# Finer early fill products and another order of the first batch's products, in strided sparse attention followed by a Mish MLP

## The chip, the cores and the metric

The kernel runs on one core of one Trainium2 chip. The metric is the device time of one execution in microseconds (us). The time before is the median of five runs. Where the text speaks of TensorE, VectorE, ScalarE, GpSimd and SyncE, the profile writes PE (and PEld for its weight loads), DVE, ACT, POOL and SP.

## The reference

Eight batches of eight heads, 576 positions, 64 values a head. Heads 0 to 3 attend to the last 32 positions ("local"), heads 4 to 7 to the earlier positions that are equal to their own modulo 32 ("strided"). The result, 4608 rows of 512, goes through an MLP with 2048 hidden values.

```python
scores = scale * np.matmul(q, k.transpose(0, 1, 3, 2))          # scale = 1/8
mask_local = (rel >= 0) & (rel < 32)                            # heads 0..3
mask_strided = (rel >= 0) & (pos[None, :] % 32 == pos[:, None] % 32)   # heads 4..7
attn = softmax(np.where(mask, scores, -1e9))
x = np.matmul(attn, v).transpose(0, 2, 1, 3).reshape(4608, 512)
h = x @ w_in                                                    # 512 -> 2048
g = h * np.tanh(np.log1p(np.exp(h)))                            # Mish
out = g @ w_out                                                 # 2048 -> 512
```

## The kernel before, in words

All data for the products is bf16, sums are fp32 in PSUM. The order of instructions on each engine is written out by hand. The MLP works on nine blocks of 512 rows: `mlp1` (line 575, then Mish at 581) makes the hidden values, `mlp2` (line 599) the output. While the MLP of block t runs, the attention of batch t+1 is put between its products. The first batch has nothing to lie beside, so its attention is a piece of its own at the start (lines 677 to 722), and this is the piece that the change touches.

The steps of this piece, in the old order:

- **Fills.** `fill` (line 547) issues products of a zeroed tile, whose result nobody reads. They keep TensorE busy while loads, copies and exponentials are on their way. Every product in this kernel, fills too, is one weight load and one matmul.
- **Transposes.** `t_step` (237) turns keys and queries of the strided heads, two heads in a step; VectorE copies the first step's result out of PSUM, ScalarE the second's. `t_step_loc0` (253) does the same for the local heads.
- **Scores.** `Attn.bias` (297) opens an accumulator with a product that writes the mask as large negative numbers; `Attn.qk` (324) adds the scores and ScalarE takes the exponential (338). The strided heads have three such rounds, ("s", 0) to ("s", 2), the local heads three, ("l", 0) to ("l", 2).
- **Pairs.** `Attn.pv2` (366, and 371 for the sum in the first batch's strided heads) multiplies two groups by the values into one accumulator; VectorE takes the reciprocal of the sums (396) and multiplies (397). There are four strided pairs and three local pairs. The first local pair needs the exponentials of ("l", 0), the second those of ("l", 0) and ("l", 1), the last those of ("l", 1) and ("l", 2).
- **Transposes of the result.** `Attn.xt` turns the attention's result into `xT`, the MLP's input: the strided halves at 420, the local halves at 410. VectorE copies the first strided one, ScalarE the others.
- **MLP1, block 0.** `mlp1(0, accs)` gives a list of steps. The first two are the "strided halves" of groups 0 and 1: four products each of 512 columns, on the strided part of `xT` alone. The next four add the local part, in pieces of 288 and 224 columns; from there on MLP1 is dense.

Three accumulators of two PSUM banks each (`acc(0)` to `acc(2)`) are shared by fills, scores, pairs and MLP. A step that takes an accumulator waits until the one that had it before is through: a fill's last product, the exponential, or the division. The tuple `accs` says which accumulators MLP1's groups take in turn.

The loads of this piece go out on GpSimd's queue in the order of use: strided keys, queries and values, local keys and queries, values, then `w_in` in five pieces, the next batch's keys and queries, and `w_out`, one piece between others.

Of the kernel before, what the change touches and what calls it, by code (L numbers as in the profile page):

```python
# [40 lines left out]
def kernel(ctx, tc, q, k, v, moe_w_in, moe_w_out, out):  # L41
# [34 lines left out]
    kTs = [const.tile([128, 16 * SU + 48], BF16, name=f"kTs{i}") for i in range(2)]  # L76
# [13 lines left out]
    def acc(i, name):  # L90

        return ps_a.tile([128, 2, 512], F32, tag=f"acc{i}", name=name)

    def tile_t(name):
        return ps_t.tile([128, 512], F32, tag="pt", name=name)


    def sT(x, b):

        return x[(b + 1) % 2 if b else 0]  # L100
# [76 lines left out]
    def cast(eng, out_, in_):  # L177
        if eng is nc.scalar:
            nc.scalar.copy(out_, in_)  # L179
        else:  # L180
            eng.tensor_copy(out_, in_)  # L181
# [48 lines left out]
    def t_step(b, which, hp, eng=None):  # L230

        eng = eng or nc.vector
        tr = tile_t("tr")[:].bitcast(BF16)
        src = (qs if which == "q" else ks)[b % 2]
        for u in range(8):
            h, jj = 2 * hp + u // 4, u % 4
            nc.tensor.transpose(  # L237
                tr[:, PN * u:PN * u + PN],
                src[0:PN, h, 128 * jj:128 * jj + 128],
                ident[0:PN, 0:PN],  # L240
            )
        dst = sT(qTs if which == "q" else kTs, b)[:, 8 * SU * hp:8 * SU * hp + 8 * SU]
        cast(
            eng, dst.rearrange("c (u n) -> c u n", u=8)[:, :, 0:PN],
            tr[:, 0:S].rearrange("c (u n) -> c u n", u=8),
        )

    def t_step_loc0(src, dst, hp, eng):

        tr = tile_t("tr")[:].bitcast(BF16)  # L250
        for j in range(CL):
            for e in range(2):
                nc.tensor.transpose(  # L253
                    tr[64 * e:64 * e + 64, PL * j:PL * j + PL], src[0:PL, 2 * hp + e, j, :],
                    ident[0:PL, 0:PL],
                )
        cast(
            eng, dst.rearrange("c (p j) -> c p j", j=CL),
            tr[:, 0:S].rearrange("c (j p) -> c p j", j=CL),
        )  # L260
# [280 lines left out]
        ]  # L541


    def fill(t, n):

        for _ in range(n):
            nc.tensor.matmul(  # L547
                t[:, 0:512], lhsT=kTs[1][:, 512:640], rhs=kTs[1][:, 0:512], start=True, stop=True
            )

    def fill_acc(i, n):
        fill(acc(i, "fill")[:, 0, :], n)

    def segs(t):
        a, e, o, r = 512 * t, 512 * t + 512, 0, []
# [6 lines left out]
    def mlp1(t, accs):  # L562
        gT = g_pool.tile([128, 16, 512], BF16, tag="gT", name="gT")

        held = {}

        def group(g, ccs=(2, 3, 0, 1), us=(0, 1), part=None):
            if g not in held:
                held[g] = acc(accs[g % 3], "psh")
            ps = held[g]  # L570
            for u in us:
                fc = 2 * g + u
                for a, n, o in segs(t) if part is None else [part]:
                    for cc in ccs:
                        nc.tensor.matmul(  # L575
                            ps[:, u, o:o + n], lhsT=w_in[:, cc, fc * 128:(fc + 1) * 128],
                            rhs=xT[:, cc, a:a + n], start=(cc == 2 and o == 0),
                            stop=(cc == 1 and o + n == 512),
                        )
            if ccs[-1] == 1 and us[-1] == 1 and (part is None or part[2]):  # L580
                nc.scalar.activation(gT[:, 2 * g:2 * g + 2, :], ps[:], AF.Mish)  # L581
        if t == 0:
            parts = (0, 288, 0), (288, 224, 288)
            return gT, [lambda g=g: group(g, (2, 3)) for g in range(2)] + [
                lambda g=g, p=p: group(g, (0, 1), part=p) for p in parts for g in range(2)
            ] + [lambda g=g: group(g) for g in range(2, 8)]
        return gT, [lambda g=g, c=c: group(g, c) for c in ((2, 3), (0, 1)) for g in range(3)] + [
            lambda g=g, u=u: group(g, us=(u,)) for g in range(3, 8) for u in range(2)
        ]
# [46 lines left out]
    with tc.manual_schedule():  # L636
        Po, Dv, Sc = nc.gpsimd, nc.vector, nc.scalar
# [37 lines left out]
        cast(Dv, ks[0][0:PN, 0:2, :], k32[0:PN])  # L675

        a = Attn(0)
        fill_acc(2, 11)
        for hp in range(2):
            t_step(0, "k", hp, Sc if hp else Dv)  # L680
        a.bias("s", 0, 0)
        fill_acc(2, 3)
        for hp in range(2):
            t_step(0, "q", hp, Sc if hp else Dv)
        a.bias("s", 1, 1)
        fill_acc(2, 1)
        a.bias("s", 2, 2)
        for i in range(3):
            a.qk([("s", i)], i)
        fill(tile_t("fill"), 2)  # L690
        a.pv2("s", 0, 0)
        t_step_loc0(kl0, kTl[:, 0, 32:32 + S], 0, Sc)
        t_step_loc0(kl0, kTl[:, 1, 32:32 + S], 1, Sc)
        a.pv2("s", 2, 1)
        a.pv2("s", 4, 2)
        fill_acc(0, 1)
        t_step_loc0(ql0, qTl[:, 0, :], 0, Sc)
        t_step_loc0(ql0, qTl[:, 1, :], 1, Sc)
        a.pv2("s", 6, 0)
        for i in range(2):  # L700
            a.bias("l", i, i + 1)
            a.qk([("l", i)], i + 1)
        for hp in range(2):
            rows_v_loc01(0, hp, Dv)
# [2 lines left out]
        a.xt("s", 0, Dv)  # L707
        a.xt("s", 1)
        fill_acc(0, 2)
        a.bias("l", 2, 0)  # L710
        a.qk([("l", 2)], 0)
        Sc.preload_act_table(AF.Mish)
        a.pv2("l", 0, 1)
        fill_acc(2, 2)
        a.pv2("l", 2, 0)
        a.pv2("l", 4, 1)
        accs = (2, 0, 1)
        gT, g1 = mlp1(0, accs)
        g1.pop(0)()
        a.xt("l", 0)  # L720
        g1.pop(0)()
        a.xt("l", 1)
# [23 lines left out]
        for t in range(NBLK):  # L746
# [4 lines left out]
            if t == 0:  # L751
# [4 lines left out]
                out_accs, accs = (z, x), (y, z, x)  # L756
            else:
# [13 lines left out]
                out_accs, accs = (z, y), (z, x, y)  # L771
# [61 lines left out]
```

## Time and profile before

| | us |
|---|---|
| median of 5 runs | 308.26 (307.45 to 309.38) |
| the profiled execution's own time | 309.47 |
| its span | 307.7 |
| TensorE busy | 299.2 (97%) |
| ScalarE busy | 181.5 |
| VectorE busy | 156.4 |
| GpSimd busy | 103.6 |
| first fill to the end of the fourth strided pair (start of the local mask products) | 1.27 to 14.57 |
| first 288-column product of MLP1 | 23.73 |

A row of the timeline gives start, length, engine, line, operation, output and inputs, the shape as rows times columns of the weights and then rows and columns of the moving operand, and a count; in brackets stands the idle time of the engine before it and what ended it. "issue" means that nothing the profile shows ended it. The length of a matmul includes its way through the array, so the distance between two starts says more of its cost than its length. The page's row for the granted clock shows full speed in all slices; the record of the clock in the trace begins at 7.3 us of the span, and the products before it start at twice the later distance.

### The profile page before, as it was taken

The page shows a single profiled execution, that of the slowest core. Times are in us where ns is not written, and L with a number is a line of the kernel's source. Part 1 is how long each engine was busy: PE and PEld are TensorE (multiplying, and loading weights), DVE is VectorE, ACT ScalarE, POOL GpSimd, SP SyncE. Part 2 cuts the span into 40 slices and gives each one's busy share as a digit, 9 for nine tenths or more (in the row PEclk, how much of TensorE's full clock was granted, in tenths as well). Part 3 has the DMA queues.
Part 4 walks back from the last instruction along what each step waited for, and adds up shares of the span by engine and source line. Part 5 has one row for each costly group of instructions (what it writes and reads, how often), then busy time and mean ns, then how long its engine had stood idle before and what let it go on. Part 6 is the DMA issues. An engine that isn't in the chain of part 4 may idle for free.

```text
span 307.7 us, 5966 instructions
## 1 busy us (share of the span) xinstructions
PE 299.2 (97%) x2474; PEld 157.0 (51%) x2474; DVE 156.4 (51%) x375; ACT 181.5 (59%) x193; POOL 103.6 (34%) x119
## 2 busy tenths in 40 slices
PE   8979999999999998999999999999999999999995
PEld 3645555544554445444579654445444544444444
DVE  4454256400860076479787978797879760000000
ACT  2656634767447663668766876687668846216501
POOL 8652329950480235004860279027600000000000
PEclk9999999999999999999999999999999999999999
DMA  8999999999999999999776998897530020011011
GB/s 135 165 203 202 203 174 128 148 150 255 167 204 135 224 185 195 119 205 190 116 127 137 194 181 169 167 192 132 109 107 0 29 110 2 0 68 70 0 67 69
DMA packets 97550, 41.81 MB, mean 136 GB/s; under 512 B 79604, under 2 KB 91460, under 8 KB 97524
## 3 DMA queue, kind: packets, MB, share of 16 engines
q1 hardware_dynamic: 71708, 28.84, 52.2%
q0 software_dynamic: 25504, 12.31, 34.1%
q8 instruction: 19, 0.31, 0.6%
q10 hardware_dynamic: 312, 0.28, 0.3%
q14 instruction: 7, 0.06, 0.1%
HBM read 36.82 MB, written 9.44 MB: 150 GB/s over the span
## 4 chain that ended last, share of the span: by engine, by line
PE 93%; DVE 3%; issue 1%; ACT 1%; ACTq 0%
PE psh L575 40%; PE pso L599 34%; PE po L366 5%; PE pso L626 5%; PE ps L324 4%; PE fill L547 2%; DVE x_l L383 1%; PE ps L297 1%; PE tr L237 1%; PE tr L253 1%; PE trx L410 1%; ACT Ps L338 1%; DVE x_s L383 1%; DVE Pl L346 1%; DVE rden L382 1%
## 5 line engine op out<-in xcount | busy, mean ns | idle before, releaser
L575 PE MATMUL psh<-xT,w_in 128*128 128x512 bf16 (+3 forms) x648 | 130.6, 355 | 0.3 <-ACT Ps L338 0.3
L599 PE MATMUL pso<-w_out,gT 128*128 128x512 bf16 x512 | 121.7, 379 | 0.0
L581 ACT ACTIVATE gT<-psh 128x1024 bf16<-128x1024 f32 x72 | 72.5, 1024 | 46.1 <-PE psh L575 46.1
L575 PEld LDWEIGHTS <-w_in 128*128 128x128 bf16 x648 | 60.7, 98 | 54.8 <-issue 0.5
L599 PEld LDWEIGHTS <-gT 128*128 128x128 bf16 x512 | 45.4, 98 | 46.1
L445 DVE STREAM_TRANSPOSE xs_t<-x_s 32x512 bf16<-32x512 bf16 x48 | 33.7, 702 | 0.9
L606 ACT COPY osb<-pso 128x1024 f32<-128x1024 f32 x16 | 17.6, 1098 | 24.8 <-PE pso L599 14.4
L382 DVE RECIPROCAL rden<-po 72x4 f32<-72x4 f32 (+1 forms) x98 | 17.3, 177 | 28.3 <-PE po L366 28.1
L181 POOL CAST kl<-kl 96x768 bf16<-96x768 f32 x10 | 8.4, 864 | 68.8 <-DMA kl<-in_k_dram 58.3
L436 DVE STREAM_TRANSPOSE xT<-x_l 32x384 bf16<-32x384 bf16 x48 | 27.3, 569 | 0.7
L181 DVE COPY osb<-pso 128x512 f32<-128x512 f32 (+1 forms) x2 | 1.1, 558 | 51.3 <-PE pso L626 51.3
L346 DVE TENSOR_TENSOR Ps<-Ps,consts_sb 72x864 bf16<-72x864 bf16 (+3 forms) x12 | 6.6, 551 | 40.0 <-ACT Ps L338 40.0
L383 DVE TENSOR_TENSOR x_s<-po,rden 72x256 bf16<-72x256 f32 x56 | 23.5, 421 | 1.9
L338 ACT ACTIVATE Ps<-ps 72x864 bf16<-72x864 f32 (+3 forms) x21 | 17.4, 861 | 11.1 <-PE ps L324 11.0
L366 PEld LDWEIGHTS <-Ps 72*128 72x128 bf16 x256 | 15.6, 97 | 11.6 <-DVE Ps L346 0.8
L452 ACT COPY xT<-xs_t 128x576 bf16<-128x576 bf16 x8 | 21.4, 2936 | 0.0
L338 ACT ACTIVATE Pl<-ps 128x960 bf16<-128x960 f32 (+1 forms) x20 | 17.3, 876 | 4.1 <-PE ps L324 3.9
L383 DVE TENSOR_TENSOR x_l<-po,rden 96x256 bf16<-96x256 f32 x42 | 17.7, 420 | 1.4
L366 PE MATMUL po<-vs,Ps 72*128 72x65 bf16 (+1 forms) x256 | 18.1, 194 | 0.1
L179 ACT COPY xT<-trx 128x576 bf16<-128x576 bf16 x15 | 9.6, 639 | 13.9 <-PE trx L420 10.0
L181 POOL CAST vl<-vl 128x768 bf16<-128x768 f32 (+2 forms) x20 | 15.5, 774 | 3.3 <-DMA vl<-in_v_dram 2.3
L346 POOL TENSOR_TENSOR Ps<-Ps,consts_sb 72x1008 bf16<-72x1008 bf16 (+1 forms) x9 | 14.5, 1637 | 2.7 <-DVE x_l L383 1.5
(93 smaller groups left out, 241.4 us busy)
## 6 DMA issues: line engine op xcount, KB each, us to landing
out_dram<-osb SPq DMA_DIRECT2D x16, 512.0 KB, 4.3
kl<-in_k_dram SPq DMA_DIRECT2D x5, 576.0 KB, 6.9
ql<-in_q_dram SPq DMA_DIRECT2D x5, 576.0 KB, 11.6
vs<-in_v_dram SPq DMA_DIRECT2D x5, 576.0 KB
vl<-in_v_dram SPq DMA_DIRECT2D x5, 576.0 KB, 9.0
w_out<-in_moe_w_out_dram POOLq DMA_DIRECT2D x4, 512.0 KB, 16.5
ks<-in_k_dram POOLq DMA_DIRECT2D x7, 288.0 KB, 9.1
qs<-in_q_dram POOLq DMA_DIRECT2D x7, 288.0 KB, 9.4
```

The lines of the kernel that those rows point to most:

```text
L181: eng.tensor_copy(out_, in_)
L338: nc.scalar.activation(pt[0:n, :, 0:nw], t[0:n, :, o0:o0 + nw], AF.Exp, scale=scale)
L346: meng.tensor_tensor(out=pm, in0=pm, in1=mk[0:n, :].unsqueeze(1).unsqueeze(1).to_broadcast([n, 2, nu, w]), op=ALU.mult,)
L366: nc.tensor.matmul(po[:, h, 0:rhs.shape[-1]], lhsT=pt[0:n, c0:c0 + 128], rhs=rhs, start=True, stop=True,)
L382: nc.vector.reciprocal(rden[0:m, :], po[0:m, :, D])
L383: nc.vector.tensor_tensor(out=dst.rearrange("p (h d) -> p h d", h=4), in0=po[0:m, :, 0:D], in1=rden[0:m, :].unsqueeze(2).to_broadcast([m, ...
L436: nc.vector.transpose(dst[32 * q:32 * q + 32, :, :, m:m + 32], src[m:m + 32, :, :, q, :])
L445: nc.vector.transpose(xs_t[32 * q:32 * q + 32, :, :, m:m + 32], src[m:m + 32, :, :, q, :])
L452: nc.scalar.copy(xT[:, 2 + c, t0:t0 + S].rearrange("p (n j) -> p j n", j=CS), xs_t[:, :, c, 0:PN])
L575: nc.tensor.matmul(ps[:, u, o:o + n], lhsT=w_in[:, cc, fc * 128:(fc + 1) * 128], rhs=xT[:, cc, a:a + n], start=(cc == 2 and o == 0), stop= ...
L581: nc.scalar.activation(gT[:, 2 * g:2 * g + 2, :], ps[:], AF.Mish)
L599: nc.tensor.matmul(p[:, ot % 2, :], lhsT=gT[:, fc, 128 * ot:128 * ot + 128], rhs=w_out[:, fc, :], start=(fc == 0), stop=(fc == 15),)
```

## The change

`fill` and `fill_acc` get a width. In the first batch's piece:

- the 11 opening fills of 512 columns become 88 of 64 columns; the two key transposes are written out with a fill of 512 between them;
- two fills become three after the strided scores; one becomes two ahead of the local query transposes;
- both local mask products come ahead of both local score groups;
- the first local pair goes ahead of the third local mask product and score round;
- the two fills between the first and second local pair are gone; the second pair takes accumulator 2 instead of 0;
- `accs` is (1, 2, 0) instead of (2, 0, 1), the first strided half of MLP1 goes ahead of the last local pair, and that pair takes accumulator 0 instead of 1.

```diff
-    def fill(t, n):
+    def fill(t, n, w=512):
         for _ in range(n):
             nc.tensor.matmul(
-                t[:, 0:512], lhsT=kTs[1][:, 512:640], rhs=kTs[1][:, 0:512], start=True, stop=True
+                t[:, 0:w], lhsT=kTs[1][:, 512:640], rhs=kTs[1][:, 0:w], start=True, stop=True
             )
-    def fill_acc(i, n):
-        fill(acc(i, "fill")[:, 0, :], n)
+    def fill_acc(i, n, w=512):
+        fill(acc(i, "fill")[:, 0, :], n, w)
...
         a = Attn(0)
-        fill_acc(2, 11)
-        for hp in range(2):
-            t_step(0, "k", hp, Sc if hp else Dv)
+        fill_acc(2, 88, 64)
+        t_step(0, "k", 0, Dv)
+        fill_acc(2, 1)
+        t_step(0, "k", 1, Sc)
         a.bias("s", 0, 0)
...
-        fill(tile_t("fill"), 2)
+        fill(tile_t("fill"), 3)
         a.pv2("s", 0, 0)
...
         a.pv2("s", 4, 2)
-        fill_acc(0, 1)
+        fill_acc(0, 2)
         t_step_loc0(ql0, qTl[:, 0, :], 0, Sc)
         t_step_loc0(ql0, qTl[:, 1, :], 1, Sc)
         a.pv2("s", 6, 0)
         for i in range(2):
             a.bias("l", i, i + 1)
+        for i in range(2):
             a.qk([("l", i)], i + 1)
...
         a.xt("s", 0, Dv)
         a.xt("s", 1)
         fill_acc(0, 2)
+        a.pv2("l", 0, 1)
         a.bias("l", 2, 0)
         a.qk([("l", 2)], 0)
         Sc.preload_act_table(AF.Mish)
-        a.pv2("l", 0, 1)
-        fill_acc(2, 2)
-        a.pv2("l", 2, 0)
-        a.pv2("l", 4, 1)
-        accs = (2, 0, 1)
+        a.pv2("l", 2, 2)
+        accs = (1, 2, 0)
         gT, g1 = mlp1(0, accs)
         g1.pop(0)()
+        a.pv2("l", 4, 0)
         a.xt("l", 0)
         g1.pop(0)()
         a.xt("l", 1)
```

## The prediction, made before the change was run

> **What bounds the kernel now.** I read the page first, for which engine sets the end and whether the loss is at one place:
>
> ```profile
> span 307.7 us, 5966 instructions
> PE 299.2 (97%) x2474; PEld 157.0 (51%) x2474; DVE 156.4 (51%) x375; ACT 181.5 (59%) x193; POOL 103.6 (34%) x119
> q8 instruction: 19, 0.31, 0.6%
> PE 93%; DVE 3%; issue 1%; ACT 1%; ACTq 0%
> ```
>
> TensorE (PE) is busy 97% of the span and carries 93% of the chain, so a microsecond of PE time saved in the front is a microsecond off the end, if no later wait takes it back. The third line matters below: 19 packets, 0.31 MB in all, 16 KB each, bring instructions. Second, the view of waits, PE alone, in the first 24 us, all that the change touches:
>
> ```profile
> PE ps L324 <- issue: 1.7, 1, 1.7
> PE fill L547 <- DVE kTs L651: 1.3, 1, 1.3
> PE po L366 <- DVE x_l L397: 0.3, 1, 0.3
> ```
>
> One wait stands out, and "issue" says that no semaphore ended it. Third, PE's timeline, for its place (start, length, count):
>
> ```profile
> 5.94 1.17 PE L237 MATMUL tr<-consts_sb,ks 72*128 72x72 bf16 x16
> ...
> 15.99 0.34 PE L324 MATMUL ps<-qTl,kTl 64*128 64x96 bf16 x8
> 17.99 0.22 PE L324 MATMUL ps<-qTl,kTl 64*128 64x96 bf16 x2 [1.65 <-issue]
> 18.14 0.69 PE L420 MATMUL trx<-consts_sb,x_s 72*128 72x72 bf16 x16
> 18.67 0.60 PE L547 MATMUL fill<-kTs 128*128 128x512 bf16 x2
> 19.32 0.33 PE L297 MATMUL ps<-consts_sb 128*128 128x192 bf16 x2
> ```
>
> The 1.65 us fall inside one group of ten products on tiles that were ready. Fourth, the DMA view for 15.2 to 16.6 us:
>
> ```profile
> q0 software_dynamic: 495, 0.26, 135.9%
> q8 instruction: 1, 0.02, 5.6%
> ```
>
> The first of the 19 instruction packets lies here: it begins at 15.32 and takes 1.26 us, behind the loads of q0. I read the stall as PE running out of instructions. Counting records in the trace: 449 PE and PEld records lie ahead of the stall, 4,981 in all, so a packet holds some 4981/19 = 262. If a packet is asked for when one packet's worth has been used up, the first request came near record 190, at 11.3 us: 4.0 us of queueing, 1.26 of transfer and 1.41 until PE went on at 17.99, 6.65 in all. The second packet fits: asked for at 17.95, it began at 21.59 and took 0.89; with 1.41 behind it that is 5.9. Later packets begin at records 703, 1009, 1276, 1500, about one a packet's worth, and come long before they are needed. Only in the front does PE use 260 instructions in 5 us.
>
> **The change part by part**, on PE's path from the first fill to MLP1's dense part, which starts at 23.73 (the first 288-column product).
>
> *88 products of 64 columns for 11 of 512.* Same 5,632 columns. The old fills start 427 ns apart, 512 columns at half rate; from about 7.3 us on they start 215 apart. The transposes at 5.94 follow the last of them directly. At 53.3 ns the new ones end at 1.27 + 88 x 53.3 = 5.96, as before. Bounds per product: 53.3 by columns; above, the 65-column products with 128 rows start 33 ns apart at full rate, and if that is array cycles, 65 at half rate. A cost at half rate pushes other work past 7.3 us, where it takes half as long, so half is refunded: 0 to +0.5. Transposes of 72 columns, each with a load, start exactly 60.0 = 72/1.2 apart in the slow stretch; they are the nearest row and point to the columns. I take 55 ns: **+0.07**.
>
> *What it adds in instructions.* 77 more products are 154 more records by the end of the fills, 158 with the two other early fills. The first request then comes at the end of the first transposes, 6.4 us instead of 11.3, and the 449th record falls at the start of the third strided pair, about 13.0. Even with the old 6.65 the packet is usable at 13.05; and at 6 to 8 us the DMA share is 1.18, against 2.35 at 12 to 14. So the first stall goes: **-1.65**, bounds -1.65 and 0. Next is the second packet: asked for at 13.0, usable 5.9 to 6.65 later, 18.9 to 19.7; record 705 comes at 20.1, in the last local pair. Margin 0.4; if the queueing were 1 us longer, 0.6 of the gain returns.
>
> *A fill between the first two transpose steps*, 512 columns on the path. All up to 7.3 us runs at half rate with or without it, so it costs its length at full rate: **+0.22**. The keys for the second step land at 6.05, no wait.
>
> *A third fill ahead of the first strided pair.* PE waits there for the exponentials: two fills from 10.41, then idle from 10.83 until 11.14. A third of 0.215 fits into that 0.3: **0**; without the cover 0.22.
>
> *A second fill ahead of the query transposes.* PE has no idle time there (13.18 to 14.57 is unbroken): **+0.22**. Its accumulator is free, the first pair's division ends at 12.70.
>
> *Local scores.* Both mask products now precede both score groups. PE's sum stays, one change of shape goes (-0.08). The first local exponential moves from 15.59 to 16.46 (0.44 from the fills, 0.43 from the mask product), the second ends at 18.37.
>
> *First local products ahead of the third score round, two fills out, strided half ahead of the last pair.* Old sum from 14.11 (fourth strided pair) to 23.73 without the stall: 7.97. The new one, from the same rows, starting 0.44 later:
> - out: two fills, 0.43; the wait for the division before the last pair (21.23 less the 20.73 when PE was through), 0.49; 0.21 between the last fill's start-up slot and the mask product at 19.32, which waits for its own accumulator's fill (18.89 + 0.38): the first local pair now lies there.
> - in: the first strided half takes accumulator 1, so it waits for the first local division: pair issued to 18.08, DVE 18.28 to 19.19 (0.20 + 0.69, as at 20.24). It also reads both strided transposes; the second's copy on ACT is queued behind the second exponential, 18.37 to 18.98. PE is through the second pair at 18.79, so it idles until 19.24: +0.45. Queued behind it are the last pair and both local transposes, nothing else.
> - The last pair (20.10) waits for the third exponential, which ends 19.47; the transposes at 20.37 and 21.49 for divisions that end 20.03 and 21.45. No further wait.
>
> Sum: -0.43 - 0.49 - 0.21 - 0.08 + 0.45 = **-0.77** (rounded). The rotated accumulators alone cost nothing: each later use comes after the last division.
>
> **Total**: +0.07 - 1.65 + 0.22 + 0.22 - 0.77 = -1.9; the dense part starts at about 21.8. Is it kept? Loads do not move with PE. The first weight columns land at 17.81 (needed 19.24), the next at 18.94 (20.6), the next batch's keys at 29.13 (needed 32.0 instead of 33.9), the first output weights at 33.32 (35.0), its values at 35.26 (35.7): all hold, the last just so. After that the waits are several us clear. So the profiled execution, 309.47 with a span of 307.7, would be 307.6 with 305.8; it stands 1.2 above the median of 308.26, from which the same 1.9 gives 306.4.
>
> The Trainium skill ("Runtime: NRT & Kernel Launch", instruction fetch mechanics) speaks against the main term: it gives PE room for 2,048 instructions, refilled in 16 KiB blocks, and calls the cost of a boundary mostly hidden. The 16 KB agrees with this trace; a store of 2,048 would not run dry after some 449 records, so the stall would be something else and stay, and the sum would be -0.3, or 308.0. I go by the row.
>
> **The rivals.**
> *The refill still comes late* (or the stall is no refill): all or part of 1.65 stays, at 13.0 or 20.1 instead of 16.3. For: the margins are 0 to 1 us, and DMA is busy throughout. Against: the earlier request and the emptier queue. -0.3 to -1.4: 306.9 to 308.0.
>
> *Slower: the weight load paces each small product.* Each comes with its own load, 151 ns in the slow stretch and 98 later. If every product waited for it, 40 would be done by 7.3, the other 48 take 4.7 and end at 12.0; the mask product starts at 12.75 instead of 7.35, so +5.4 - 2.0 = +3.4: 311.7. At c ns apart in the slow stretch (half later) the shift is 44c - 2.3 us with c in us; the forecast falls under 0.5% from 63 ns, and the kernel is slower by 0.5% from 133 ns. Against: loads of 138 ns hide behind transposes 60 apart. The skill ("TensorE: Matmul & The Clock Gate", LDWEIGHTS) would have a load of 128 columns take 107 ns: by that the sum would be about +0.5. No row here shows such spacing.
>
> *The clock rises later.* It rises at 7.3, 6 us after the first fill. If small products count for less and it rises 3 us later, work done in that time at half rate costs 1.5: 307.9.
>
> **How the numbers follow.** Forecast 0.62, 305.5 to 307.0 at the bounds of the fill cadence and a division more or less; late refill 0.22; weight load 0.10; later clock 0.06. About 0.5% (1.5 us) is what a measurement can tell: faster is below 306.7, four fifths of the forecast, 0.51; same is the rest of it, the late refill and the clock, 0.39; slower 0.10. The range, 305.4 to 308.4, leaves out the weight load and the tails.
>
> **What would show it.** Right: no PE gap marked "issue" above 0.3 us before 24 us; the first instruction packet near 9 to 11 us; 64-column products 53 to 56 ns apart, ending near 6.0; the strided half waiting some 0.4 for a division or the copy; the first 288-column product near 21.8. Wrong: an "issue" gap near 13 or 20 us, the fills ending after 7, or the clock rising after 8.

## The result and the profile after

The changed kernel takes 306.36 us (median of 35 runs) against 307.85 for the kernel before (59 runs beside them): a ratio of 0.995, 95% interval 0.9938 to 0.9962, or 1.5 us less (1.2 to 1.9). The prediction said 306.4, from a gain of 1.9 and a median of 308.26 over five runs of the kernel before.

The profiled execution took 306.21 us with a span of 304.4, which is 3.3 us under the profiled execution of before: more than twice the difference of the medians. The page's first lines:

```profile
span 304.4 us, 6124 instructions
PE 298.4 (98%) x2552; PEld 159.7 (52%) x2552; DVE 155.8 (51%) x375; ACT 181.2 (60%) x193; POOL 102.7 (34%) x119
q8 instruction: 20, 0.33, 0.5%
PE 94%; DVE 3%; issue 1%; ACT 1%; ACTq 0%
```

The 78 more products are there (2552 for 2474), one more instruction packet, and TensorE (PE) is 0.8 us less busy over the whole span. The view of PE's waits in the first 24 us has no "issue" left, but a new small wait of MLP1's first strided half for the first local division:

```profile
PE fill L547 <- DVE kTs L651: 1.3, 1, 1.3
PE psh L575 <- DVE rden L396: 0.3, 1, 0.3
```

PE's timeline at the start and around the old stall (start, length):

```profile
1.27 4.87 PE L547 MATMUL fill<-kTs 128*128 128x64 bf16 x88 [1.27 <-DVE kTs L651]
5.95 0.56 PE L237 MATMUL tr<-consts_sb,ks 72*128 72x72 bf16 x8
...
15.42 0.60 PE L324 MATMUL ps<-qTl,kTl 64*128 64x96 bf16 x20
15.95 0.69 PE L420 MATMUL trx<-consts_sb,x_s 72*128 72x72 bf16 x16
16.48 0.60 PE L547 MATMUL fill<-kTs 128*128 128x512 bf16 x2
16.92 0.42 PE L366 MATMUL po<-vl,Pl 128*128 128x65 bf16 x8
17.18 0.33 PE L297 MATMUL ps<-consts_sb 128*128 128x192 bf16 x2
17.43 0.26 PE L324 MATMUL ps<-qTl,kTl 64*128 64x96 bf16 x4
17.73 0.42 PE L366 MATMUL po<-vl,Pl 128*128 128x65 bf16 x8
18.45 1.02 PE L575 MATMUL psh<-xT,w_in 128*128 128x512 bf16 x4 [0.29 <-DVE rden L396]
...
20.98 0.41 PE L575 MATMUL psh<-xT,w_in 128*128 128x288 bf16 x2
```

All 20 local score products run through without a gap, and the dense part of MLP1 starts at 20.98 instead of 23.73. The first instruction packet begins at 8.18 us (15.32 before).

One profile of each kernel says little on sizes here, as further profiles of the same two kernels showed. So I cut the front in two at the fourth strided pair and read these numbers from every profile. "Stage" is from there (the start of the pair's second product, 0.04 us behind the first) to the first 288-column product, "rest" from that product to the end; the clock column is the start of full speed by the clock's record (for the first profile of the changed kernel, which has none, by the spacing of its products):

| kernel | full clock | first packet, begin + length | "issue" gap | 4th pair | stage | dense part | rest |
|---|---|---|---|---|---|---|---|
| before, 1st | 7.3 | 15.32 + 1.26 | 1.65 | 14.16 | 9.58 | 23.73 | 284.0 |
| before, 2nd | 6.5 | 13.98 + 1.60 | 0.51 | 14.32 | 8.44 | 22.76 | 284.5 |
| before, 3rd | 7.2 | 13.74 + 1.44 | none | 14.96 | 7.75 | 22.71 | 283.1 |
| changed, 1st | 6.2 | 8.18 + 0.95 | none | 14.11 | 6.87 | 20.98 | 283.5 |
| changed, 2nd | 4.2 | 8.41 + 0.89 | none | 14.12 | 6.87 | 20.99 | 283.1 |
| 64-column fills alone | 4.6 | 8.85 + 0.94 | none | 14.27 | 7.75 | 22.02 | 283.4 |
| changed, 512-column fills | 5.9 | 13.58 + 1.60 | 0.70 | 14.11 | 7.77 | 21.87 | 283.1 |
| changed, three fills out | 5.5 | 9.15 + 0.94 | none | 14.65 | 6.87 | 21.52 | 283.1 |
| changed, last pair first | 6.8 | 8.24 + 0.89 | none | 14.48 | 7.05 | 21.53 | 283.1 |
| changed, first pair late | 5.8 | 8.16 + 0.94 | none | 14.11 | 7.55 | 21.66 | 283.1 |

Six of these profiles have a gap of 0.16 us marked "issue" beside a fill at 10 to 12 us, which the table leaves out: there the record of one fill is missing. The second profile of before, for example, has 2,435 records of products for 2,474 of weight loads. A count of records is therefore good to one or two.

### The profile page after: what moved, and what is told of

Read it like the earlier page. It is cut to its first block, busy times and chain, and to the rows that moved or that the text cites. A ratio compares the mean times of both kernels' runs of the same rounds, so it can differ in the third digit from the quotient of the medians.

```text
span 304.4 us, 6124 instructions
## 1 busy us (share of the span) xinstructions
PE 298.4 (98%) x2552; PEld 159.7 (52%) x2552; DVE 155.8 (51%) x375; ACT 181.2 (60%) x193; POOL 102.7 (34%) x119
## 4 chain that ended last, share of the span: by engine, by line
PE 94%; DVE 3%; issue 1%; ACT 1%; ACTq 0%
PE psh L575 41%; PE pso L599 35%; PE po L366 5%; PE pso L626 5%; PE ps L324 4%; PE fill L547 3%; DVE x_l L383 1%; PE trx L410 1%; PE tr L237 1%; PE tr L253 1%; PE ps L297 1%; DVE x_s L383 1%; PE trx L420 1%; DVE rden L382 0%; ACT Ps L338 0%
## 5 line engine op out<-in xcount | busy, mean ns | idle before, releaser
L346 DVE TENSOR_TENSOR Ps<-Ps,consts_sb 72x864 bf16<-72x864 bf16 (+3 forms) x12 | 8.1, 673 | 40.0 <-ACT Ps L338 40.0
```

The source lines that it names most:

```text
L346: meng.tensor_tensor(out=pm, in0=pm, in1=mk[0:n, :].unsqueeze(1).unsqueeze(1).to_broadcast([n, 2, nu, w]), op=ALU.mult,)
```

## The experiments

Three theories were on the table. R: PE ran out of instructions, and earlier records bring the refill forward. C: small products raise the clock earlier. O: the new order makes the gain.

### The 64-column fills alone

```diff
 # the kernel before
-        fill_acc(2, 11)
+        fill_acc(2, 88, 64)
```

> The kernel before with one edit: the 11 opening fills of 512 columns become 88 of 64, order and all other fills as before. Theory R (PE ran out of instructions, earlier records bring the refill forward): first instruction packet at 8 to 10 us instead of 15.3, no 'issue' gap over 0.3 us on PE before 24 us, first 288-column product at 22.0 instead of 23.7, time 1.2 to 1.8 us under the kernel before. Theory C (the gain comes from the clock, which small products raise earlier): clock at 6 us, 0.5 us under before, and an issue gap of 1 us or more still somewhere before 20 us. Theory O (the new order makes the gain): within 0.3 us of before.

Measured: 307.13 against 307.87 of before, ratio 0.9974 (0.9954 to 0.9995). First packet at 8.85, no gap, stage 7.75, dense part at 22.02: R's picture in every place, but R's size of 1.2 to 1.8 us became 0.7 (0.15 to 1.4 by the interval). The clock rose early too (4.6), and it brought nothing: the fourth pair came at 14.27, no earlier than in the first profile of before, as the waits show that PE then stands before the key cast and the query load.

```profile
PE tr L237 <- DMA qs<-in_q_dram: 0.6, 1, 0.6
PE tr L237 <- DVE ks L181: 0.4, 1, 0.4
```

### The 512-column fills back in the changed kernel

```diff
 # the changed kernel
-        fill_acc(2, 88, 64)
+        fill_acc(2, 11)
```

> The changed kernel with the 11 opening fills of 512 columns put back; order and the other fills stay changed. Theory R: the first packet again near 15 us, an issue gap of 1.3 to 1.7 us near 16 us among the local scores, 0 to 0.7 us under the kernel before and 1.2 to 1.8 over the changed kernel. Theory C: no issue gap, clock at 7.3 us, 0.6 over the changed kernel. Theory O: as fast as the changed kernel within 0.3 us.

Measured: 307.55, ratio to before 0.9978 (0.9953 to 1.0003). The stall is back at the same place, among the local scores, with 0.70 us:

```profile
16.64 0.29 PE L324 MATMUL ps<-qTl,kTl 64*128 64x96 bf16 x5 [0.70 <-issue]
```

1.1 us over the changed kernel run beside it (306.47): against O, and below the 1.2 that R expected, as the stall is half of R's 1.3 to 1.7. But O is right in part: without its stall this kernel's stage is 6.87 too (7.77 less the 0.70 and the 0.2 that such a gap costs besides, see below), so the new order has a gain of its own, beside the one that R explains.

### How large the stall is in the kernel before

Two more profiles of the unchanged kernel.

> The kernel before, profiled once more, for the size of its stall in another execution. Theory R with a size that varies: an issue gap on PE in front of about the 449th record, near 16 us, between 0 and 1.7 us, as long as the first packet's end plus 1.4 us lies behind the moment when PE is through with that record; the stage from the fourth strided pair to the first 288-column product takes 7.75 us plus the stall (7.75 is what the kernel with only the 64-column fills took). Theory P (the 1.65 us of the first profile are typical): 1.4 us or more.

> As the run above, a third sample: theory R with a varying size 0 to 1.7 us, theory P 1.4 or more. The stage is again 7.75 us plus the gap.

Measured: 0.51 us in the second profile and no gap in the third; theory P, that 1.65 was typical, falls. Here is the line of the second, and then a wait of the third that the first did not have:

```profile
17.01 0.22 PE L324 MATMUL ps<-qTl,kTl 64*128 64x96 bf16 x2 [0.51 <-issue]
```

```profile
PE tr L237 <- DMA qs<-in_q_dram: 0.7, 1, 0.7
```

In the third profile the packet ended at 15.18, 1.4 us earlier than in the first (16.58), and PE, held 0.7 us by the query load, reached record 449 some 0.8 us later: the packet was there. So both sides vary, and here the earlier packet is the larger part. What PE loses before a late load comes off the stall. The kernel before with another place for a GpSimd cast (the last of the experiments, far behind the front) gives a fourth sample of the same front, with 0.15 us at the same record:

```profile
16.25 0.22 PE L324 MATMUL ps<-qTl,kTl 64*128 64x96 bf16 x2 [0.15 <-issue]
```

A gap here costs 0.2 more than its length: 1.65 makes the stage 1.83 longer than 7.75, 0.51 makes it 0.69, and 0.15 makes it 0.33 longer. The mean over the four is 0.7 us. The 64-column fills alone bring 0.7 in time; the two agree, but four executions between 0 and 1.8 do not fix the size closely.

### Half as many and twice as many

```diff
 # the kernel before
-        fill_acc(2, 11)
+        fill_acc(2, 44, 128)      # and, in the other kernel, fill_acc(2, 176, 32)
```

> The kernel before with 44 opening fills of 128 columns: half of the added records (66 of 154). Theory R, counting records: the first packet is asked for at about 9.5 us and begins at 11.5 to 13.5, PE is through with record 449 at about 14.6, in or just ahead of the fourth strided pair, so an issue gap there of 0 to 1.8 us and none at 16 us. Theory S (the stall belongs to the local scores, whatever the count): the gap stays in the local scores near 16 us.

> The kernel before with 176 opening fills of 32 columns: 330 records more than before, twice what the change adds. If they run by columns they end at 6.0 us as well. Theory R: the first packet is asked for within the fills at 3.8 us and is there by 10; the second is asked for at about 9.8 us, usable 5.9 to 6.7 us later at 15.7 to 16.4, and needed at record 705, about 14.4 us: an issue gap of 1.2 to 2.0 us near 14.4, so more small products are worse than 88. Theory C (small products raise the clock or fill PE better, the more the better): no gap, as fast as with 88 or faster. If small products have a floor per product over 27 ns in the slow stretch, the fills end later than 6.0, by 2.3 us at 40 ns.

The gap moved to where the count said, from the local scores into the fourth strided pair, and with 176 products to the second packet's border:

```profile
16.25 0.16 PE L371 MATMUL po<-vl,Ps 72*128 72x1 bf16 x1 [1.88 <-issue]
```

```profile
15.10 0.16 PE L371 MATMUL po<-vl,Ps 72*128 72x1 bf16 x1 [0.44 <-issue]
```

The records of PE and PEld ahead of the gap were 449 and 448 in the kernel before (449 in its fourth sample), 447 in the one with 512-column fills put back, 447 here with 44 products and 703 with 176. The gap moves through the program, and the count stays at 447 to 449 or lies one packet further on: this settles R against S. It speaks against C as well: with 44 products the clock rose at 4.7 us, earlier than in any profile of before, and the kernel was no faster. The end of the gap obeys one rule as well: PE goes on 1.3 to 1.5 us after the end of the packet that it needs (16.58 to 17.99; 15.58 to 17.01; 14.96 to 16.25; 15.18 to 16.64; 14.86 to 16.25; 13.56 to 15.10). Half the added records moved the stall and did not shorten it: 309.58 in the one run, against 308.30 for the kernel before beside it, also one run. Twice as many cost 0.44 at the second border, less than the 1.2 to 2.0 expected, as that packet queued 2.3 us only; its products start 27 ns apart, by columns, with no floor.

### The three added fills

```diff
 # the changed kernel
-        fill_acc(2, 1)                   # between the key transposes
...
-        fill(tile_t("fill"), 3)
+        fill(tile_t("fill"), 2)
...
-        fill_acc(0, 2)                   # ahead of the local query transposes
+        fill_acc(0, 1)
```

> The changed kernel without the three fills it adds (the one between the key transposes, the third one after the strided scores, the second one ahead of the local query transposes). By the prediction's sum the first and the last cost 0.22 us each and the middle one nothing: 0.44 us under the changed kernel, first 288-column product 0.4 us earlier, if the clock has risen by then. Theory F (they are needed, as the clock or the refill depends on them): the same time as the changed kernel or above it, with a later clock or an issue gap.

> The changed kernel once more, beside the others on one chip. Expected 1.5 us under the kernel before, with no issue gap before 24 us; the start of the clock's full speed within 5.5 to 7.5 us.

Measured: 306.26 without them, 306.47 with them, ratios to before 0.9951 (0.9927 to 0.9975) and 0.9962 (0.9937 to 0.9988): no difference that can be told, and the 0.44 expected would not show either. Against the expectation, the clock of the second profile of the changed kernel rose at 4.2. Without the fills the fourth strided pair came later, not earlier (14.65 against 14.12), with two waits for loads:

```profile
PE tr L237 <- DMA qs<-in_q_dram: 0.5, 1, 0.5
PE tr L253 <- DMA lq<-in_k_dram: 0.4, 1, 0.4
```

The second wait is chance: the local keys landed at 12.11 in this execution, against 11.35 in the other. The other profiles price the fills better. Ahead of the query transposes, the eight profiles without the fill between the key transposes have a wait for the query load of 0.27 to 0.96 us, all but the first of before; the six with it wait 0.16 or less. So that fill mostly lies in a wait. From the third to the fourth strided pair, the eight profiles with one fill take 1.38 us and the six with two take 1.59: the fill ahead of the local query transposes costs its 0.21, as predicted. From the strided scores to the first pair all fourteen take 1.35, so the third fill there costs nothing, also as predicted.

### The two parts of the new order

```diff
 # the changed kernel: the last local pair first
+        a.pv2("l", 4, 0)
         g1.pop(0)()
-        a.pv2("l", 4, 0)
...
 # the changed kernel: the first local pair late
-        a.pv2("l", 0, 1)
         a.bias("l", 2, 0)
         a.qk([("l", 2)], 0)
         Sc.preload_act_table(AF.Mish)
+        a.pv2("l", 0, 1)
```

> The changed kernel with the last local pair ahead of MLP1's first strided half again (accumulators as changed). Stage from the fourth strided pair to the first 288-column product, without an issue gap: 6.87 us in the changed kernel. If the strided half fills the wait for the third exponential: PE idles some 0.65 us before the last pair and the stage is 7.1. If the term is nothing: 6.87.

> The changed kernel with the first local pair behind the third local score round again, without the two fills that followed it. The mask product waits for its fill again (0.2 us) and the first division starts 0.66 later, with it the strided half: stage 7.5 us. If the strided half waits for the transposes' copy or the weights instead: 6.9 to 7.1.

Stages 7.05 and 7.55, against 6.87. The waits are the ones expected, first of the one kernel, then of the other:

```profile
PE po L366 <- ACT Pl L338: 0.5, 1, 0.5
```

```profile
PE psh L575 <- DVE rden L396: 0.9, 1, 0.9
```

So the early strided half is worth 0.18 us, the early first pair 0.68. The stage is the right yardstick for such terms: it repeats to the hundredth between profiles whose clock and loads differ (6.87 three times in the table, 7.75 twice), while single times of the two kernels (306.38 and 306.50) tell nothing.

### An overlap far from the change

The rest is 0.9 and 1.4 us longer in the first two profiles of before than in the third, and most of it is one wait of PE, of 0.7 and 1.2 us. Just ahead of it VectorE's mask product, some 94 us after the first 288-column product, runs beside GpSimd's cast of batch 4's strided values and is stretched to 1.53 and 2.02; alone it takes 0.65 (third profile). From the second profile of before, VectorE and GpSimd (start, length), then PE's wait in 100 to 128 us:

```profile
116.44 2.02 DVE L346 TENSOR_TENSOR Pl<-Pl,consts_sb 128x960 bf16<-128x960 bf16 x1
```

```profile
116.06 1.90 POOL L181 CAST vs<-vs 72x2048 bf16<-72x2048 f32 x1 [3.77 <-DMA vs<-in_v_dram]
```

```profile
PE trx L420 <- DVE x_l L383: 1.2, 1, 1.2
```

In both of these profiles the cast began first. In the changed kernel the mask product was over 0.4 us (first profile) and 2.9 us (second) before the cast began. In the profile with 44 products it began 0.27 us ahead of the cast and kept its 0.65, while the cast took 2.13 in place of 1.90. That profile's rest was 284.0 all the same, so the rest has other causes too. I tried to move the cast away, in both kernels:

```diff
-                if t < 3:
+                if t == 2:
+                    cast_v_loc(t + 2, Po)
+                    cast(Po, vs[0][0:PN, :, :, 0:D], vs32[0:PN])
+                elif t < 3:
                     cast_v(t + 2, Po, Po)
```

> The changed kernel, and in block 2 GpSimd casts batch 4's local values ahead of its strided values instead of behind them. Theory K (a GpSimd cast beside VectorE's mask product at about 94 us after the first 288-column product stretches that from 0.65 to 1.5 to 2.0 us and PE waits 0.7 to 1.2): the cast leaves that place, the rest from the first 288-column product to the end is 283.1 us in the profile, and as the changed kernel mostly escapes the overlap already, the time is 0 to 0.3 us under it. If the swap makes the strided values late: a PE wait at about 104 us after that product, and slower.

> The kernel before with the same swap. Theory K: the rest is 283.1 us whatever the stall in the front was (it was 284.0 and 284.5 in two of three profiles of the kernel before), and the time is 0.3 to 0.7 us under the kernel before. Without K: as the kernel before within 0.2 us, and a rest of 284 us as often as before.

It did the opposite, in the way that was named as the other possibility, and by more than foreseen: 311.95 for the changed kernel, ratio to before 1.0123 (1.0088 to 1.0159). The strided values are late, and PE waits:

```profile
PE po L366 <- POOL vs L181: 3.3, 1, 3.3
```

The rest grew by 7.0 us (290.1), more than twice the wait. The windows from 112 to 150 us say why (stretch, its length, then busy time and count of PE, PEld, DVE, ACT and POOL, the granted clock, DMA share, GB/s):

```profile
112.00:127.60 15.60, 12.23 (x132) 6.46 (x131) 8.09 (x23) 8.25 (x11) 5.70 (x8) 1.00 1.25 194
127.60:134.60 7.00, 6.28 (x29) 2.74 (x29) 1.88 (x7) 1.33 (x2) 0.67 (x1) 0.51 0.95 202
134.60:150.00 15.40, 15.40 (x118) 7.55 (x117) 12.43 (x25) 10.78 (x14) 4.55 (x6) 1.00 1.28 180
```

In the wait the clock dropped to half, and it stayed there for 6.8 us (127.69 to 134.52), which costs another 3.4 by an estimate (half of 6.8). The kernel before with the swap has runs of both kinds, 306.7 to 309.4 and 312.3 to 316.3 us; its profile is of the second, with a wait of 3.8 us and the same fall of the clock, and the comparison of the first kind (1.0015, 0.9987 to 1.0043) decides nothing. So no run shows what the overlap alone costs. How often the overlap strikes the kernel before, and so its part in the medians, stays open.

## Why the prediction was right

The median fell where it was put, 306.36 for 306.4, and by the mechanism that was named. The closeness is luck: the gain was 1.5 and not 1.9, and the median of 308.26 that 1.9 was taken from lay 0.4 above the 307.85 of the 59 runs. Two terms were wrong in size, with errors of +0.9 and -0.2.

- **The stall, -1.65.** Right that PE ran out of instructions, that the count of records decides, and that 154 more records bring the packet in time; it began at 8.18, even ahead of the 9 to 11 expected. The size was read from one execution. Four profiles gave 1.65, 0.51, 0 and 0.15, and the edit alone is worth 0.7 us (0.15 to 1.4 by its interval). The size depends on two things that vary: how long the packet queues behind loads, and how late the loads make PE.
- **The second packet.** Predicted usable at 18.9 to 19.7, needed at 20.1. It begins at 16.20 in the first profile, so with its 0.94 and the 1.4 it is usable at 18.5; PE came to record 705 at 19.3. No stall; the margin is 0.8.
- **The small products, +0.07.** They start 53 ns apart and end at 5.95. The weight load does not pace them, so the slower rival had no ground. The Trainium skill's 107 ns for a load ("TensorE: Matmul & The Clock Gate", LDWEIGHTS) does not show in the spacing of 53.
- **The added fills, +0.44.** Half of it. The one ahead of the local query transposes costs 0.21, as priced. The one between the key transposes was priced from one execution with a late clock. The clock rose between 4.2 and 7.3 us over the profiles; when it is early, PE stands before the query load, and this fill lies in that wait. The price of a fill is the price of what would be late otherwise, and that was not asked for this one.
- **The order, -0.77.** -0.88 by the stage (7.75 to 6.87); both stages were predicted 0.2 to 0.3 too long (7.97 and 7.20), the difference holds. Its parts were put at 0.2 and 0.6 before their runs, and are 0.18 and 0.68.
- **The sum** with what was measured: -0.7 + 0.2 - 0.88 = -1.4; the medians say -1.5. The first term is known to 0.6 at best, so the agreement is no closer than that.
- **Kept to the end.** Yes: the rest is no longer than before. What was not seen is that the rest itself varies by up to 1.4 us between executions, in part with the overlap above. The 3.3 us between the two first profiles are 1.83 from the stall, 0.88 from the order, 0.5 from the rest and 0.05 ahead of the fourth pair.
- **The late clock** did not occur: 4.2 to 6.8 us with 64 columns, 5.9 to 7.3 with 512. Whether small products raise it earlier can't be told from so few. The Trainium skill ("TensorE: Matmul & The Clock Gate", the HAM clock gate) has a window that runs free of the kernel's start, so that the moment varies. The moment does vary here, but by 3.1 us, where the page puts it at half a microsecond to either side.
- **The skill on instructions** ("Runtime: NRT & Kernel Launch", instruction fetch mechanics) had room for 2,048 instructions on PE. The gaps at records 447 to 449 and at 703 in six profiles say that PE here had far less ahead, and that a border is not always hidden.

## What to carry to other kernels

A stall that ends on no semaphore, in the middle of products whose inputs are ready, is a question for the instruction packets: count the records ahead of it in two variants, and if the count stays while the place moves, it is the refill. Finer products early, where PE has nothing to do anyway, bring the refill forward; half the dose, in its one run, only moved the stall. Before pricing a wait from one profile, take two more: here 1.65 us was some 0.7, while the length of a stage between two fixed points repeated to the hundredth and priced the new order.

## What the runs showed of the hardware

- PE goes on 1.3 to 1.5 us after the end of the instruction packet it waits for (six gaps). By the estimate that a packet is asked for when one packet's worth of records is used up, the first packet begins 1.6 to 4.0 us after that in the front of these kernels (from record 190 in each).
- A PE wait of 3.3 us in mid-kernel halved the clock for 6.8 us and so cost 3.4 us more; the gaps of 1.9 us and below in the front and the wait of 1.2 us did not.
- A VectorE mask product of 0.65 us took 1.53 and 2.02 us beside a GpSimd cast that had begun before it. Where the mask product began first it kept its 0.65 us, and the cast took 2.13 in place of 1.90 (one profile).
